# Three loads moved ahead of the entry barrier, and a 16 KB load cut into four

## The chip, the cores and the metric

The kernel runs on one core of a Trainium2 chip. The time is the device time of one execution in microseconds (us). "Span" is the time from the first to the last instruction in the profile; in the profiled runs it is 2.0 us (before) shorter than the device time. The engines are called PE (matmuls), DVE, ACT, POOL and SP; SP issues loads and stores, POOL issues the loads that cast fp32 to fp16. A load has "landed" when the last of its completions has come in. The granted clock is the share of its full clock that the record shows PE to have been allowed.

Almost all executions of this kernel agree within 1.5%. A few are some per cent longer (slow); they are used for nothing that concerns the time.

## The reference

Four batches of 12480 tokens of 128 numbers go through an attention block with 32 inducing points, then through a two-layer network with an exact GELU:

```
h   = softmax(scale * inducing @ x.T) @ x      # per batch: 32 x 128
y   = softmax(scale * x @ h.T) @ h             # per batch: 12480 x 128
out = gelu(y @ w_in) @ w_out                   # 49920 x 128, fp32
```

x is 25.6 MB and so is out, both fp32 in DRAM. The inducing points are 32 rows of 512 bytes, the weights 2 MB.

## The kernel before

What matters here is the start. POOL and SP issue the first loads; PE turns the inducing points (`indT`), runs eight warm-up matmuls ("fillers"), and then transposes the first tiles of x. Everything that PE does with x comes after the inducing points.

```python
blank = consts.tile([128, 512], FP16)
nc.vector.memset(blank, 0.0)

x_first = sb.tile([128, 32, 128], FP32, tag="o", bufs=OBUFS)
x_pair = x_tile(units[0][0])
src = units[0][0].rows_of(x_rows)
nc.sync.dma_start(out=x_first[:, :16, :], in_=src[:, :16, :])     # SP, 1 MB, no cast
nc.gpsimd.dma_start(out=x_pair[:, 16:, :], in_=src[:, 16:, :])    # POOL, casts, 512 KB written
a_load(units[0][2])                                               # POOL, casts, 1 MB written

identity = consts.tile([128, 128], FP32)
make_identity(nc, identity)                                       # on POOL
...
ind_s = consts.tile([M, C], FP32)
nc.sync.dma_start(out=ind_s, in_=inducing)                        # SP, 16 KB
indT_ps = ps.tile([C, M], FP32, tag="sc", bufs=3)
nc.tensor.transpose(indT_ps, ind_s, identity[:M, :M])
...
dim = ps.tile([128, 512], FP32, tag="sc", bufs=3)

def fill():
    nc.tensor.matmul(dim, blank[:, :128], blank, start=True, stop=True)
...
p_fill = None
for i in range(FILLERS):                                          # FILLERS = 8
    p_fill = plan.add((-1, 0), {"PE": 0.427}, lambda e: fill(), [p_fill])
```

Later loads of x are issued by POOL as buffers come free; stores of results are issued by SP.

The kernel's source does not show the entry barrier; the program built from it does. A barrier is a point that no engine passes before all of them have reached it. It is made of semaphores, counters that engines raise and wait for, and of drains: a drain is an instruction that is meant to hold its engine until earlier work is done. In front of all the code above stand, on each engine:

```
ACT, PE, DVE, SP:  Drain   (then: gather += 1)
                   EventSemaphore  wait release >= 1
POOL:              Memset x4       (small constants)
                   Drain
                   EventSemaphore  wait gather >= 4
                   EventSemaphore  release += 4
```

So POOL opens the barrier, and only after its own drain. (The profile shows the drains and these waits in this order on each engine.)

## Time and profile before

| | before |
|---|---|
| device time | 134.59 us (median; 134.44 to 135.2 in 5 runs) |
| span of the profiled run | 132.8 us |
| barrier open for the other engines | 0.7 us |
| PE has the inducing points | 6.43 us |
| first transposes of x | 10.03 us |
| last store issued | 122.6 us |

The profile's lines read: start in us, duration in us, engine, line of the kernel, operation, output<-input, count, and in brackets the idle time before and what ended it. `SPq` and `POOLq` are what the sequencer of that engine does. From the timeline of the kernel before, its first 12 us:

```profile
0.35 0.10 POOL L1130 MEMSET const-uint8-127<- 128x1 uint8 x1
0.75 1.28 ACT L355 ACT_TABLE_LOAD   x1 [0.75 <-PEq L1130]
0.75 0.38 SPq L285 DMA_DIRECT2D x_first<-in_x_dram  x1
1.19 0.42 SPq L295 DMA_DIRECT2D ind_s<-in_inducing_dram  x1
1.24 0.71 POOL L286 DMA_DIRECT2D xh<-in_x_dram  x1 [0.79 <-POOLq L1130]
1.95 0.53 POOL L277 DMA_DIRECT2D xh<-in_x_dram  x1
...
3.01 1.07 POOL L277 DMA_DIRECT2D xh<-in_x_dram  x2
...
6.43 0.28 PE L297 MATMUL indT_ps<-identity,ind_s 32*128 32x32 f32 x1 [6.43 <-DMA ind_s<-in_inducing_dram]
6.65 3.59 PE L349 MATMUL dim<-blank 128*128 128x512 f16 x8
...
10.03 2.07 PE L367 MATMUL tr<-identity_h,xh 128*128 128x128 f16 x32
```

The barrier opens at 0.7 us, SP issues x_first at once and the inducing points right behind it, and PE waits for those until 6.43 us. POOL's line for a load lasts 0.5 to 0.7 us, although the data comes many microseconds later. The Trainium skill ("Perfetto Trace Analysis", Per-engine timelines, DMA Instruction — SWDGE (GPSIMD)) says why: the profile ends such a line when the descriptors are written, not when the data has moved. This trace agrees: the first of POOL's loads, 0.71 us long from 1.24 us, landed at 8.58 us.

The table of stretches for the same kernel: the stretch in us and its length, then the busy time of PE, PE's weight loads, DVE, ACT and POOL (with counts), the granted clock, the DMA share (1 is all 16 DMA engines busy) and GB/s:

```profile
12.00:15.00 3.00, 1.34 (x28) 0.63 (x27) 1.67 (x4) 1.98 (x5) 0.53 (x1) 1.00 1.05 218
15.00:17.00 2.00, 2.00 (x46) 1.79 (x46) 1.25 (x2) 0.00 (x0) 0.00 (x0) 1.00 0.96 201
94.00:106.00 12.00, 10.19 (x142) 4.80 (x139) 10.92 (x32) 9.76 (x26) 7.63 (x8) 1.00 1.01 425
122.60:132.80 10.20, 0.00 (x0) 0.00 (x0) 0.24 (x2) 0.00 (x0) 0.00 (x0) 0.50 0.60 249
```

The DMA engines are never idle between 4 and 128 us. (218 GB/s of casting loads is the same work as 425 GB/s of stores: fp32 is read, half the bytes are written.) After the last store is issued, at 122.6 us, 10.2 us go by: the queue still holds the stores before it.

### The profile page before, as it was taken

How to read it: one execution, taken by the hardware profiler on the slowest of the kernel's cores; microseconds unless marked ns; L12 is line 12 of the kernel's file. 1: busy time of each engine (PE TensorE's matmuls, PEld its weight loads, DVE VectorE, ACT ScalarE, POOL GpSimd, SP SyncE). 2: the span in 40 equal slices, each digit the busy share in tenths (PEclk: the TensorE clock that was granted, in tenths of full speed). 3: DMA queues.
4: the chain of work that ended last, by engine and by line, in shares of the span. 5: the costliest groups of instructions: out<-in, count | busy, mean ns of one | idle time of the engine just before them, and what ended most of it. 6: DMA issues, size and time to landing. Idle time of an engine off the chain costs nothing. (4 is left out here: it accounts for less than half of the span.)

```text
span 132.8 us, 3490 instructions
## 1 busy us (share of the span) xinstructions
PE 97.3 (73%) x1365; PEld 56.6 (43%) x1365; DVE 93.4 (70%) x266; ACT 76.2 (57%) x173; POOL 65.3 (49%) x85
## 2 busy tenths in 40 slices
PE   0098678449999999999697979957988779295000
PEld 0036545349465556665363555624544424131000
DVE  1086557323699998999999489749989999998000
ACT  3004273316866879598878458967779759174000
POOL 6920131119344646894824409914167999556000
PEclk9999999965899999999999999999999999955555
DMA  4999999999999999999999999999999999999970
GB/s 123 302 223 215 217 200 220 212 220 210 220 205 220 215 200 313 333 398 367 299 318 348 266 227 324 321 412 425 430 423 426 415 437 413 411 434 425 421 300 15
DMA packets 5666, 40.17 MB, mean 303 GB/s; under 512 B 624, under 2 KB 1936, under 8 KB 2192
## 3 DMA queue, kind: packets, MB, share of 16 engines
q0 software_dynamic: 2848, 13.30, 49.5%
q1 hardware_dynamic: 2800, 26.63, 48.3%
q8 instruction: 11, 0.18, 0.5%
q14 instruction: 7, 0.06, 0.1%
HBM read 27.67 MB, written 25.56 MB: 401 GB/s over the span
## 5 line engine op out<-in xcount | busy, mean ns | idle before, releaser
L686 POOL TENSOR_TENSOR pair<-pair,rr 128x512 f32<-128x512 f32 x29 | 30.3, 1056 | 29.1 <-ACT pair L355 19.9
L670 PE MATMUL at<-q,e 128*128 128x512 f16 (+1 forms) x104 | 33.5, 389 | 7.2 <-DVE o L701 2.4
L367 PE MATMUL tr<-identity_h,xh 128*128 128x128 f16 x392 | 29.3, 227 | 2.3 <-DMA xh<-in_x_dram 2.1
L701 DVE TENSOR_TENSOR pair<-at,rr 128x512 f32<-128x512 f32 x41 | 26.8, 679 | 3.1 <-DMA out_dram<-pair 1.6
L367 PEld LDWEIGHTS <-xh 128*128 128x128 f16 x392 | 24.5, 102 | 7.6 <-issue 3.5
L355 ACT ACTIVATE xT<-tr 128x1024 f16<-128x1024 f16 (+1 forms) x17 | 16.7, 981 | 19.1 <-PE tr L367 19.1
L353 DVE COPY xT<-tr 128x1024 f16<-128x1024 f16 (+1 forms) x35 | 21.9, 644 | 7.0 <-PE tr L367 6.7
L355 ACT ACTIVATE pair<-at 128x512 f32<-128x512 f32 x29 | 17.2, 598 | 3.1 <-PE at L670 1.7
L628 ACT ACTIVATE e<-s 128x512 f16<-128x512 f32 (+1 forms) x28 | 15.2, 563 | 6.4 <-PE s L616 5.2
L277 POOL DMA_DIRECT2D xh<-in_x_dram x15 | 8.3, 556 | 21.5 <-DMA xh<-in_x_dram 14.3
L393 ACT ACTIVATE e<-s 128x512 f16<-128x512 f32 (+1 forms) x28 | 15.2, 543 | 5.4 <-PE s L381 5.0
L670 PEld LDWEIGHTS <-e 128*128 128x128 f16 (+1 forms) x104 | 8.9, 105 | 11.5 <-issue 8.5
L415 PE MATMUL hun<-xh,e1t 128*32 128x128 f16 x392 | 10.5, 222 | 3.2 <-DVE e1t L407 3.0
L562 POOL TENSOR_TENSOR pt<-pt 128x512 f32<-128x512 f32 (+4 forms) x20 | 12.0, 601 | 1.5
L407 DVE STREAM_TRANSPOSE e1t<-e 128x256 int32<-128x256 int32 (+1 forms) x28 | 11.0, 399 | 2.2 <-ACT e L393 2.2
L381 PE MATMUL s<-xT,indT 128*32 128x512 f16 (+1 forms) x108 | 10.5, 376 | 1.6 <-ACT xT L355 0.8
L415 PEld LDWEIGHTS <-e1t 128*32 128x32 f16 x392 | 6.3, 96 | 11.5 <-DVE e1t L407 9.0
L701 DVE TENSOR_TENSOR o<-at,rr 128x512 f32<-128x512 f32 (+1 forms) x19 | 10.2, 558 | 0.9 <-PE at L670 0.7
L686 POOL TENSOR_TENSOR o<-o,rr 128x512 f32<-128x512 f32 x8 | 8.2, 1044 | 4.0 <-ACT o L355 2.3
L616 PE MATMUL s<-xT,hT 128*32 128x512 f16 (+1 forms) x100 | 9.7, 391 | 0.1
L640 PEld LDWEIGHTS <-e 128*128 128x128 f16 (+1 forms) x104 | 5.6, 99 | 5.0 <-issue 1.3
L640 PE MATMUL r<-strand,e 128*128 128x4 f16 (+1 forms) x104 | 6.9, 168 | 0.2 <-ACT e L393 0.2
(72 smaller groups left out, 93.0 us busy)
## 6 DMA issues: line engine op xcount, KB each, us to landing
out_dram<-pair SPq DMA_DIRECT2D x9, 2048.0 KB, 15.0
xh<-in_x_dram POOLq DMA_DIRECT2D x11, 1024.0 KB, 28.0
out_dram<-o SPq DMA_DIRECT2D x6, 1024.0 KB, 7.5
x_first<-in_x_dram SPq DMA_DIRECT2D x1, 1024.0 KB, 5.4
xh<-in_x_dram POOLq DMA_DIRECT2D x1, 512.0 KB, 7.3
w_in_h<-in_moe_w_in_dram POOLq DMA_DIRECT2D x1, 512.0 KB, 17.5
w_out_h<-in_moe_w_out_dram POOLq DMA_DIRECT2D x1, 512.0 KB, 19.5
out_dram<-o SPq DMA_DIRECT2D x4, 96.0 KB, 12.4
```

Source lines behind the costliest of these rows:

```text
L353: nc.vector.tensor_copy(out=out, in_=in_)
L355: nc.scalar.activation(out=out, in_=in_, func=AF.Copy)
L367: nc.tensor.transpose(tr[:, c - c0, : u.p], xh[: u.p, c, :], identity_h[: u.p, : u.p])
L393: nc.scalar.activation(out=e1[: u.p, : u.nc // 2, :, :], in_=s1[: u.p, : u.nc, :].rearrange("r (a b) i -> r a i b", b=2), func=AF.Exp, sca ...
L407: nc.vector.transpose(out=pairs(e1t)[: u.p, :n], in_=pairs(e1)[: u.p, :n])
L415: nc.tensor.matmul(bt.hun[32 * j : 32 * j + 32, :], e1t[: u.p, c // 2, :, c % 2], xh[: u.p, c, :], start=u.idx == 0 and c < 4, stop=c + 4 ...
L562: nc.gpsimd.tensor_tensor(out=bt.pt[:, :, :, :half], in0=bt.pt[:, :, :, :half], in1=bt.pt[:, :, :, half : 2 * half], op=ALU.add,)
L628: nc.scalar.activation(out=e2[: u.rows, : u.cols], in_=s2[: u.rows, : u.cols], func=AF.Exp, scale=SCALE,)
L640: nc.tensor.matmul(r2[: u.p, ci, : u.nj], e2[: u.rows, ci * u.p : (ci + 1) * u.p], strand[: u.rows, : u.nj], start=True, stop=True,)
L670: nc.tensor.matmul(at[: u.p, : u.nj, :], e2[: u.rows, ci * u.p : (ci + 1) * u.p], bt.q[: u.rows, : u.nj, :], start=True, stop=True,)
L686: nc.gpsimd.tensor_tensor(out=part, in0=part, in1=rr2[: u.p, ci, : u.nj].unsqueeze(2).broadcast_to([u.p, u.nj, 128]), op=ALU.mult,)
L701: nc.vector.tensor_tensor(out=ov[: u.p, ci, :, :], in0=at[: u.p, : u.nj, :], in1=rr2[: u.p, ci, : u.nj].unsqueeze(2).broadcast_to([u.p, u. ...
```

## The change

The intent: the first three loads need nothing that the barrier protects, so let SP and POOL issue them before it, and have the DMA engines start earlier. The inducing points come in four transfers of 8 rows instead of one of 32.

```diff
     ind_s = consts.tile([M, C], FP32)
-    nc.sync.dma_start(out=ind_s, in_=inducing)
+    for m in range(0, M, M // 4):
+        nc.sync.dma_start(out=ind_s[m : m + M // 4], in_=inducing[m : m + M // 4])
@@ at the end of the kernel
+    nc.at_finalize(loads_ahead)
     return nc
+
+def loads_ahead(nc):
+    entry, body = nc.main_func.blocks[:2]
+    head, rest = list(entry.instructions), list(body.instructions)
+    for engine, n in ((mybir.EngineType.SP, 1), (mybir.EngineType.Pool, 2)):
+        moves = [i for i in rest if i.engine == engine][:n]
+        for i in moves:
+            assert isinstance(i, mybir.InstDMACopy)
+            rest.remove(i)
+        at = min(
+            k for k, i in enumerate(head)
+            if i.engine == engine
+            and isinstance(i, (mybir.InstDrain, mybir.InstMemset))
+        )
+        head[at:at] = moves
+    entry.instructions, body.instructions = head, rest
```

The moved loads land in front of the first drain or memset of their engine: on SP in front of its drain, on POOL in front of its four memsets, and so in front of its drain too.

More of the change, by code (lines that the diff above doesn't have):

```diff
@@ L977 @@
         general(tc, x, moe_w_in, moe_w_out, out, ind_s, identity)
+    nc.at_finalize(loads_ahead)
     return nc
+def loads_ahead(nc):
[7 more added lines that the diff above has]
+        at = min(
+            k
+            for k, i in enumerate(head)
+            if i.engine == engine
[3 more added lines that the diff above has]
+    entry.instructions, body.instructions = head, rest
 def general(tc, x, moe_w_in, moe_w_out, out, ind_s, identity):
```

## The prediction

> **What bounds the kernel now.** The DMA engines, end to end. The table of stretches shows a DMA share of 0.96 to 1.12 from 4 to 128 us; PE, DVE and ACT are busy 73%, 70% and 57% of the span (busy table). With casting loads counted at source size, the trace's DMA packets move 410 to 430 GB/s in every 2 us from 4 to 128 us, except 48 to 50 us (about 330). Outside it: the first packet starts at 1.76 us, 2 to 4 us run at about 285 GB/s, and one slow engine trails from 128 to 131 us. The chain of waits ends at 122.7 us; the span, 132.8 us, ends with the stores.
>
> Bytes issued less bytes moved leave at least 1.1 MB of stores queued whenever the next is issued after 94 us (2.5 us at 425 GB/s, an estimate). Moderate delays of the compute are absorbed; only the DMA engines' start counts.
>
> **What the change does, costed.**
> - SP: the 1 MB load of x_first starts at 0.75 us, after the barrier. Ahead of it, it can start when SP's register moves are done, at about 0.25 us. Its first packet came 1.0 us after issue, so I expect it at 1.25 us: gain 0.5 us.
> - POOL: its two load issues (0.71 and 0.53 us, timeline) now precede its memsets and drain. They start 0.6 us after POOL's barrier step now, so I expect them from 0.25 to 0.8 us, and the barrier released at 1.9 to 2.5 instead of 0.68 us. ACT's table load (1.28 us) and DVE's first memset slide into idle time: ACT first computes at 11.7 us, PE at 6.4 us.
> - Inducing points: one issue of 0.42 us at 1.19 us becomes four, from about 2.0-2.5 to 3.7-4.2 us. Now the rows sit behind x_first, ahead of POOL's loads, and PE gets them at 6.4 us. After the change POOL's loads are probably queued first. The Trainium skill ("DMA: Bandwidth & Descriptors", Queues, rings and completion order) says each engine takes turns between queues by packet; here the turns are long: the store issued at 45.6 us sent its first packet at 49.5 us. POOL's first load needs eight packets of 0.33 us per engine, 2.6 us. So I expect the inducing points at 6.5 to 8 us, not sooner, and the first transposes of x (10.0 us now, after 3.6 us of fillers) at 10 to 11.7 us.
>
> **On the critical path.** Only the 0.5 us of earlier DMA. The late inducing points are absorbed: PE waits for loads again at about 18.6 and at 29.0 us (1.4 us), and those come 0.5 us earlier.
>
> **Predicted time.** 134.59 - 0.5 = 134.1 us, range 133.4 to 135.0. Faster by over 2%: 0.02; within 2%: 0.94; slower by over 2%: 0.04.
>
> **What would show it right.** Timeline: x_first issued at about 0.25 us, barrier and ACT table load after 1.9 us. First packets near 1.25 us. Waits: PE's wait for the inducing points ends between 6.4 and 8 us. Stretches: DMA share about 1 from 4 us to the end; last store issued within 1 us of now; span 132.3 us.
>
> **What would make it wrong.** If the four small transfers wait two turns behind POOL's loads (the second has packets of 0.63 us, 5 us a turn), they land after 12 us, the compute falls 6 us behind, the store queue runs dry and the time rises by 2 to 3 us. If they land sooner than now, nothing more is gained. If SP's load can't start early, the gain is nil.

## More of the kernel before

The instructions of the entry barrier have one line number of their own. The view of that line (operation, count, then least, median and greatest duration in ns, first and last start in us) shows the drains:

```profile
L1130 ACTq DRAIN  x1: 8/8/8, 0.1 to 0.1; - x1
L1130 SPq DRAIN  x1: 7/7/7, 0.3 to 0.3; - x1
L1130 POOLq DRAIN  x1: 186/186/186, 0.3 to 0.3; - x1
```

They are short: POOL's took 186 ns, the others 7 to 10 ns.

## The result, and the profile after

| | before | after |
|---|---|---|
| device time, median of 5 runs | 134.59 us | 142.36 us (141.42 to 143.08) |
| span of the profiled run | 132.8 us | 139.8 us |
| barrier open for the other engines | 0.7 us | 13.3 us |
| PE has the inducing points | 6.43 us | 19.06 us |
| first transposes of x | 10.03 us | 22.66 us |
| last store issued | 122.6 us | 132.5 us |

The ratio is 1.0568 (95% interval 1.051 to 1.0626): slower by over 5%. Ratios here are the mean time of one kernel's fast runs over that of the other's fast runs of the same rounds, so not quite the ratio of the medians.

The timeline of the changed kernel, the lines that answer to those above:

```profile
0.26 0.39 SPq L285 DMA_DIRECT2D x_first<-in_x_dram  x1
0.75 0.72 POOL L286 DMA_DIRECT2D xh<-in_x_dram  x1 [0.75 <-issue]
1.46 0.54 POOL L277 DMA_DIRECT2D xh<-in_x_dram  x1
...
2.09 0.12 POOL L1154 MEMSET const-uint8-127<- 128x1 uint8 x1
13.33 0.20 POOL masks.py:197 MEMSET identity<- 128x128 f32 x1 [11.12 <-POOLq L1154]
13.34 1.36 SPq L298 DMA_DIRECT2D ind_s<-in_inducing_dram  x4
13.34 1.28 ACT L358 ACT_TABLE_LOAD   x1 [13.34 <-PEq L1154]
...
13.95 1.07 POOL L277 DMA_DIRECT2D xh<-in_x_dram  x2
...
19.06 0.28 PE L300 MATMUL indT_ps<-identity,ind_s 32*128 32x32 f32 x1 [19.06 <-DMA ind_s<-in_inducing_dram]
19.28 3.59 PE L352 MATMUL dim<-blank 128*128 128x512 f16 x8
22.66 2.41 PE L370 MATMUL tr<-identity_h,xh 128*128 128x128 f16 x32
```

The three loads do start early: x_first at 0.26 us instead of 0.75 us. Then no engine computes or issues anything between 2.2 and 13.3 us. The view of the barrier's line shows what held it:

```profile
L1154 ACTq DRAIN  x1: 8/8/8, 0.1 to 0.1; - x1
L1154 SPq DRAIN  x1: 123/123/123, 0.7 to 0.7; - x1
L1154 POOLq DRAIN  x1: 11832/11832/11832, 1.3 to 1.3; - x1
```

POOL's drain now lasts 11.83 us, from 1.26 to 13.09 us. POOL's second load, issued at 1.46 us, landed at 12.97 us. The view of DMA issues between 1.4 and 2.05 us (size, us from issue to landing) has it:

```profile
xh<-in_x_dram POOLq DMA_DIRECT2D x1, 1024.0 KB, 11.5
```

SP's drain stands behind SP's load in the same way and took 0.12 us, although that load landed only at 5.68 us.

The table of stretches of the changed kernel shows two holes in the DMA engines' work that were not there before:

```profile
12.00:15.00 3.00, 0.00 (x0) 0.00 (x0) 0.50 (x2) 1.28 (x1) 1.55 (x4) 1.00 0.02 4
15.00:17.00 2.00, 0.00 (x0) 0.00 (x0) 0.00 (x0) 0.00 (x0) 2.00 (x5) 1.00 0.93 103
100.00:112.00 12.00, 11.18 (x158) 5.66 (x157) 11.09 (x27) 9.65 (x28) 6.00 (x6) 1.00 0.62 255
132.50:139.80 7.30, 0.00 (x0) 0.00 (x0) 0.25 (x2) 0.00 (x0) 0.00 (x0) 0.50 0.69 274
```

The first hole is at 12 to 17 us: the two early loads are done, POOL issues its next one only at 13.95 us, and its first packets start at 15.21 us. The second is at 100 to 112 us: the compute, late since the start, has no result ready to store. To put numbers on it, I took the bytes of the DMA packets in a stretch (casting loads at source size), divided by 425 GB/s, and subtracted that from the length of the stretch. This is the DMA time lost:

| stretch | before, us lost | after, us lost |
|---|---|---|
| 0 to 6 us (start) | 2.63 | 2.23 |
| 6 to 20 us | 0.0 | 4.25 |
| 20 to 90 us | 0.76 | 0.22 |
| 90 us to the last store's issue | 0.0 | 5.34 |
| last store's issue to the end | 4.14 | 2.51 |
| sum | 7.50 | 14.55 |

The sums differ by 7.05 us and the spans by 7.06 us. They must, since both kernels move the same bytes; what the table tells is where the time went. The gain that was hoped for is in the first row: 0.4 us.

### The profile page after: what moved, and what is told of

The parts are those of the page before. It is cut to its first block, busy times and chain, and to the rows that moved or that the text cites. A ratio compares the mean times of both kernels' runs of the same rounds, so it can differ in the third digit from the quotient of the medians.

```text
span 139.8 us, 3494 instructions
## 1 busy us (share of the span) xinstructions
PE 96.9 (69%) x1365; PEld 56.7 (41%) x1365; DVE 93.5 (67%) x266; ACT 76.1 (54%) x173; POOL 65.8 (47%) x85
## 5 line engine op out<-in xcount | busy, mean ns | idle before, releaser
L673 PEld LDWEIGHTS <-e 128*128 128x128 f16 (+1 forms) x104 | 8.9, 105 | 11.7 <-issue 8.7
L384 PE MATMUL s<-xT,indT 128*32 128x512 f16 (+1 forms) x108 | 10.2, 366 | 1.7 <-ACT xT L358 0.8
L704 DVE TENSOR_TENSOR o<-at,rr 128x512 f32<-128x512 f32 (+1 forms) x19 | 10.2, 559 | 0.9 <-PE at L673 0.7
```

Source lines behind the costliest of these rows:

```text
L384: nc.tensor.matmul(s1[32 * j : 32 * j + 32, : u.nc, :], indT, xT[:, :, 32 * j : 32 * j + 32], start=True, stop=True,)
L673: nc.tensor.matmul(at[: u.p, : u.nj, :], e2[: u.rows, ci * u.p : (ci + 1) * u.p], bt.q[: u.rows, : u.nj, :], start=True, stop=True,)
L704: nc.vector.tensor_tensor(out=ov[: u.p, ci, :, :], in0=at[: u.p, : u.nj, :], in1=rr2[: u.p, ci, : u.nj].unsqueeze(2).broadcast_to([u.p, u. ...
```

## The experiments

Theory D: POOL's drain waits until the loads that POOL issued before it have landed; POOL opens the barrier, so the whole program starts some 12.6 us late. Rival S: the four small transfers cost the time. Rival B: any load in flight at the barrier holds it. All experiments gave correct results.

### e1: the three loads ahead, the inducing points in one transfer

```diff
-    for m in range(0, M, M // 4):
-        nc.sync.dma_start(out=ind_s[m : m + M // 4], in_=inducing[m : m + M // 4])
+    nc.sync.dma_start(out=ind_s, in_=inducing)
```

> The three loads ahead of the barrier, the inducing points in one transfer again. Theory D (POOL's drain in front of the barrier waits until its own two early loads have landed, and everything behind the barrier starts some 12.7 us late): the barrier is released at 13.3 us as in the change; the time stays at 138.5 to 142.5 us. Rival S (the four small transfers cost the time, because they take turns behind POOL's loads): the time falls to 134 to 135 us. A mix: if the split adds 3 us of the wait (PE waited to 19.06 us, though the points were issued from 13.3 us), PE's wait now ends at 15.5 to 16.5 us and the time is about 139 to 140 us.

Measured: 137.46 us (three fast runs, 137.24 to 137.56, one slow), ratio 1.022 (1.0143 to 1.0296). The barrier opens at 13.0 us, as in the change. The barrier's drain and the start of PE in the profile of e1:

```profile
L1153 POOLq DRAIN  x1: 11584/11584/11584, 1.3 to 1.3; - x1
```

```profile
14.83 0.28 PE L299 MATMUL indT_ps<-identity,ind_s 32*128 32x32 f32 x1 [14.83 <-DMA ind_s<-in_inducing_dram]
15.04 3.31 PE L351 MATMUL dim<-blank 128*128 128x512 f16 x8
18.19 1.95 PE L369 MATMUL tr<-identity_h,xh 128*128 128x128 f16 x32
```

The drain stays at 11.6 us without the split. One transfer that was issued at 13.09 us was with PE at 14.83 us; four, issued from 13.34 us, at 19.06 us. The time lies below everything that had been expected for theory D and for a mix (138.5 to 142.5 us): the barrier is as late as theory D says, but the split has a larger share than was allowed for. So the time of the change has two parts: about 3.2 us from the late barrier (137.46 against 134.27 us, the median of before in these rounds), and about 4.9 us (142.36 less 137.46 us, different rounds) that the split adds when the barrier is late. In the account of DMA time lost, e1 has 4.14 us between 6 and 20 us, like the change, but only 1.34 us from 90 us to the last store's issue (5.34 us in the change): what the split adds is the second hole.

### e2: only the split

```diff
 # the kernel before, with
+    for m in range(0, M, M // 4):
+        nc.sync.dma_start(out=ind_s[m : m + M // 4], in_=inducing[m : m + M // 4])
```

> Only the inducing points in four transfers, no load ahead. Theory D: 134.3 to 135.5 us, the barrier released at 0.7 us; PE's wait for the points may end later than the 6.4 us of before (up to 9 us), and the queue of stores absorbs that. Rival S: 138 us or more.

Measured: 134.86 us, ratio 1.0028 (0.9968 to 1.0089). PE had the points at 7.69 us instead of 6.43 us, and the time did not notice. Rival S falls as the root: the split alone costs nothing.

### e3: only SP's load ahead

```diff
-    for engine, n in ((mybir.EngineType.SP, 1), (mybir.EngineType.Pool, 2)):
+    for engine, n in ((mybir.EngineType.SP, 1),):
 # inducing points in one transfer
```

> Only the SP load of x_first ahead of the barrier, POOL's loads behind it, the inducing points in one transfer. Theory D: SP's drain does not wait for its load (it took 0.12 us in the change), so the barrier is released by 1.2 us, first data packet at about 1.25 us instead of 1.76 us, time 134.0 to 134.4 us. Rival (any load in flight holds the barrier): released at about 6 us, time 137 us or more.

Measured: 134.48 us, ratio 1.0004 (0.9954 to 1.0055). The barrier opened at 0.96 us with SP's load in flight, and SP's drain took 0.12 us again. Rival B falls: a load that SP issued does not hold the barrier. The first data packet came at 1.30 us, as expected, but the expected gain (0.2 to 0.6 us) did not show.

### e4: POOL's loads after its drain, still ahead of the barrier's semaphores

```diff
             if i.engine == engine
-            and isinstance(i, (mybir.InstDrain, mybir.InstMemset))
+            and isinstance(i, mybir.InstDrain)
         )
+        at += engine == mybir.EngineType.Pool
         head[at:at] = moves
 # inducing points in one transfer
```

> SP's load ahead as in the change, POOL's two loads placed after POOL's drain but before the two semaphore steps of the barrier; the inducing points in one transfer. Theory D: the drain finds nothing in flight and is short (about 0.2 us), the barrier is released between 0.7 and 2.5 us, time 133.8 to 134.6 us. Rival B (it is the barrier as such, or loads ahead of it, whatever the drain): released at 13 us, time 139 to 142 us.

Measured: 134.09 us (seven runs, 133.81 to 135.19), ratio 0.9967 (0.992 to 1.0014). From the view of the barrier's line in e4, and its timeline:

```profile
L1154 POOLq DRAIN  x1: 188/188/188, 0.3 to 0.3; - x1
```

```profile
7.40 0.28 PE L299 MATMUL indT_ps<-identity,ind_s 32*128 32x32 f32 x1 [7.40 <-DMA ind_s<-in_inducing_dram]
```

The same loads, behind POOL's memsets and drain instead of in front of them, and the drain is back to 188 ns; the barrier opens at 1.61 us and the whole loss is gone. This is the experiment that settles the root: it is the order of POOL's loads and POOL's drain, not the loads' being ahead of the barrier. (The loads also pass the four memsets, but in the change those had ended at 2.21 us, with 10.9 us of drain still to come.)

### e5: only the smaller of POOL's two loads ahead of the drain

```diff
-    for engine, n in ((mybir.EngineType.SP, 1), (mybir.EngineType.Pool, 2)):
+    for engine, n in ((mybir.EngineType.SP, 1), (mybir.EngineType.Pool, 1)):
 # inducing points in one transfer
```

> Only POOL's first load (half the size of the second) ahead of its drain, with SP's load; the inducing points in one transfer. Theory D: the drain ends when that load has landed, so the barrier is released at 8.0 to 8.6 us (in e1, with both loads, 13.1 us; the first alone had landed at 7.9 us there), time 135 to 137 us. Rival (the drain has a fixed long cost once any POOL load precedes it): 13 us again, 137.5 us.

Measured: 137.23 us, ratio 1.0209 (1.0151 to 1.0267). The barrier's line, and the issue of that load (size, us from issue to landing):

```profile
L1153 POOLq DRAIN  x1: 6935/6935/6935, 0.8 to 0.8; - x1
```

```profile
xh<-in_x_dram POOLq DMA_DIRECT2D x1, 512.0 KB, 6.9
```

The load was issued at 0.75 us and landed at 7.68 us; the drain ended at 7.76 us. In e1 the second load landed at 12.72 us and the drain ended at 12.84 us. The drain follows the landing of the last load in front of it by about 0.1 us, wherever that is, so the rival's fixed cost falls. The time lay just above what was expected: POOL's second load now goes out only behind the barrier, and the DMA engines are short of work from 7 to 11 us (3.6 us lost between 6 and 20 us).

### e6: a POOL drain behind the barrier, that only POOL feels

```diff
     make_identity(nc, identity)
+    nc.gpsimd.drain()
 # otherwise the kernel before
```

> The kernel before with one POOL drain put in its body, behind the barrier, after the first two loads and the making of the identity. Nothing ahead of the barrier. Theory D: the drain lasts from about 3 us until the second load has landed at about 13.3 us, POOL's later loads are issued only then, the DMA engines run dry between about 12.5 and 15 us and the time rises by 2.5 to 4 us to 137 to 138.5 us, although the first transposes of x stay at 10 us. Rival (only the late start of the compute costs time, the late loads nothing): 134 to 135 us.

Measured: 137.96 us, ratio 1.0241 (1.0178 to 1.0304). The drain in the view of its line, POOL's next load, and two stretches:

```profile
L291 POOLq DRAIN  x1: 10465/10465/10465, 2.7 to 2.7; - x1
```

```profile
13.71 1.07 POOL L277 DMA_DIRECT2D xh<-in_x_dram  x2 [10.63 <-issue]
```

```profile
12.00:15.00 3.00, 1.27 (x21) 0.58 (x22) 1.92 (x4) 2.29 (x5) 1.29 (x3) 1.00 0.16 25
...
94.00:106.00 12.00, 10.98 (x160) 5.76 (x160) 11.08 (x28) 9.79 (x27) 6.25 (x7) 1.00 1.02 430
```

The drain needs no barrier to do this: it lasted from 2.74 to 13.21 us, and the load in front of it landed at 13.09 us. The first transposes of x stayed at 9.8 us, so the compute was on time; only POOL's later loads were late. That alone cost 3.3 us of span, and the first hole accounts for it: 3.5 us lost between 6 and 20 us, none during the stores. The queue of loads was emptied, and what is not moved then has to be moved later.

### e7 and e8: only the compute late

```diff
+    extra = [1] * 12          # e8: [1] * 30
     def fill():
         nc.tensor.matmul(dim, blank[:, :128], blank, start=True, stop=True)
+        while extra:
+            extra.pop()
+            nc.tensor.matmul(dim, blank[:, :128], blank, start=True, stop=True)
```

> The kernel before with 12 more warm-up matmuls on PE, so that only the compute starts late, by 5.1 us (first transposes at 15.2 us), and the loads stay as they are. If the queue of stores absorbs it (about 4 to 5 us, read from the change against e1): 134.3 to 135.5 us. If the compute is the bound from the start: 139 us or more.

> The same with 30 more warm-up matmuls: the compute alone 12.8 us late (first transposes at 22.8 us, as in the change), the loads on time. If about 4.6 us are absorbed, 142 to 144 us with the store queue dry at about 100 to 106 us; if the DMA bytes alone bound the time, 134 to 136 us.

The doses were smaller than planned. I had reckoned 0.43 us for a warm-up matmul, but only the first nine came every 0.43 us; from 3.8 us after the first one on they came every 0.22 us. The Trainium skill ("TensorE: Matmul & The Clock Gate", Part 1: The HAM clock gate) says that PE runs at half clock until it has been busy for about 3.4 us, half a microsecond more or less. These traces agree roughly: 3.8 us after the first warm-up matmul in e7 and e8, 2.9 us in e1. So the transposes of x began at 12.63 us in e7 (2.6 us late) and at 16.52 us in e8 (6.5 us late).

Measured: e7 134.86 us (three fast runs, one slow), ratio 1.0063 (0.9979 to 1.0148), not to be told from before. e8 139.12 us, ratio 1.0354 (1.0285 to 1.0423). Two stretches of e8:

```profile
98.00:107.00 9.00, 8.44 (x129) 4.35 (x118) 8.21 (x20) 6.74 (x18) 3.76 (x5) 1.00 0.62 255
...
129.60:137.10 7.50, 0.00 (x0) 0.00 (x0) 0.19 (x2) 0.00 (x0) 0.00 (x0) 0.50 0.65 260
```

In e8 all loads were on time (no more DMA time lost before 20 us than before), yet the same second hole opened at 98 to 107 us. So the compute's late start alone is enough to open the second hole. The size shows in when the last store is issued and how long the program runs on from there:

| | transposes of x from | last store issued | from there to the end | span |
|---|---|---|---|---|
| before | 10.0 | 122.6 | 10.2 | 132.8 |
| e7 | 12.6 | 122.7 | 10.0 | 132.7 |
| e6 | 9.8 | 126.5 | 9.5 | 136.1 |
| e8 | 16.5 | 129.6 | 7.5 | 137.1 |
| e1 | 18.2 | 128.4 | 7.3 | 135.8 |
| after | 22.7 | 132.5 | 7.3 | 139.8 |

(All in us, from the profiled run of each.) Where the DMA queue is full, the last store has to queue and 10 us follow it. Where it has run dry, 7.3 to 7.5 us follow. So, where no DMA time was lost at the start, a last store that is up to about 2.8 us late costs nothing: in e2 it was issued at 124.7 us, 2.1 us late, and the span was 132.3 us. Where the queue has run dry, what goes beyond that counts in full: after, 9.92 us late less 2.86 us is the 7.06 us of the span; e8, 6.95 us late less 2.63 us, 4.3 us. In e6 the queue was full and the span longer all the same, because of the hole at the start.

How late the last store is does not follow from the start of the compute alone: e7 began 2.6 us late and issued its last store 0.1 us late; e1 began 1.7 us later than e8 and issued its last store 1.1 us earlier. What lies between was not tested, nor was the full delay of 12.6 us with the loads on time.

### e9: the change with POOL's loads after its drain, split included

```diff
 # the change, with e4's edit of the place; four transfers of 8 rows
```

> The change as it is, four transfers of the inducing points included, but POOL's two loads placed after its drain (as in e4). If the drain is the root and the split only costs what it does because the late barrier puts it against POOL's large packets: barrier released at about 1.6 us, PE gets the inducing points at 8 to 10 us, time 134.0 to 135.3 us. If the split has a cost of its own of 4 to 5 us (change against e1): 138 to 139 us.

Measured: 133.98 us (three fast runs, one slow), ratio 0.9984 (0.9942 to 1.0025). From its view of waits (who waited for what: us in total, times, longest us):

```profile
PE indT_ps L300 <- DMA ind_s<-in_inducing_dram: 9.6, 1, 9.6
```

The four transfers made PE wait to 9.65 us instead of the 7.40 us of e4, and that was absorbed. The split costs time only where the late barrier has used up the slack.

### e10: as e4, and the inducing points issued by ACT ahead of its drain

```diff
-    nc.sync.dma_start(out=ind_s, in_=inducing)
+    nc.scalar.dma_start(out=ind_s, in_=inducing)
-    ((mybir.EngineType.SP, 1), (mybir.EngineType.Pool, 2))
+    ((mybir.EngineType.SP, 1), (mybir.EngineType.Activation, 1), (mybir.EngineType.Pool, 2))
 # with e4's edit of the place
```

> As e4, and the inducing points (one transfer) issued by ACT ahead of its drain, so that they go beside x_first instead of behind it. PE should have them at 3 to 5 us, the first transposes of x at 8 to 9 us, set by PE's fillers and DVE's setup. If the DMA engines bound the time: 133.6 to 134.4 us, no more than 0.5 us gained. If an earlier compute is worth its microseconds: 132.5 us or less.

Measured: 133.88 us (six runs, 133.47 to 135.18), ratio 0.9954 (0.9922 to 0.9986). This is the only version whose interval lies below 1: it beats the kernel before by about 0.5%, and the change by 6% (median against median, different rounds). The start of PE in its profile:

```profile
2.98 0.29 PE L299 MATMUL indT_ps<-identity,ind_s 32*128 32x32 f32 x1 [2.98 <-POOL identity masks.py:199]
3.20 3.60 PE L351 MATMUL dim<-blank 128*128 128x512 f16 x8
8.30 3.43 PE L369 MATMUL tr<-identity_h,xh 128*128 128x128 f16 x32 [1.51 <-DMA xh<-in_x_dram]
```

PE now waits for the identity, not for the points, and later for x itself. Which of the two, the earlier DMA start or the earlier compute, gave the half per cent was not separated. Its profiled run was the slowest of the six (135.18 us), so its lines show the start, not the gain.

### e11: the change with two transfers of 16 rows

```diff
-    for m in range(0, M, M // 4):
-        nc.sync.dma_start(out=ind_s[m : m + M // 4], in_=inducing[m : m + M // 4])
+    for m in range(0, M, M // 2):
+        nc.sync.dma_start(out=ind_s[m : m + M // 2], in_=inducing[m : m + M // 2])
```

> The change with two transfers of 16 rows instead of four of 8. Theory T (the rows that reach the engines after POOL's third load, whose first packets started at 15.2 us in the change, take turns with its packets of 8 KB; those before it do not): the second transfer is issued at about 13.7 us, its rows go at about 14.7 us, before POOL's packets; PE has the points by 15.0 to 15.6 us, time 137 to 138.3 us, as e1. Rival F (each further small transfer costs a fixed time, 4.2 us for three): about 16.3 us and 139 us.

Measured: 137.91 us (three fast runs, 137.27 to 137.92; two slow), ratio 1.0255 (1.0216 to 1.0295), as e1. PE had the points at 15.13 us (the profiled run fell in the slow state; only this early time is used from it). Theory T predicted 15.0 to 15.6 us, rival F 16.3 us.

The packets of the change's trace fit theory T. The four transfers were issued at 13.34, 13.74, 14.07 and 14.40 us. Of the 32 rows, 22 had gone when POOL's first 8 KB packet started at 15.21 us, two went at 16 us, and the last eight only at 17.27 to 17.93 us, with their completions at 17.93 to 18.6 us. A completion there came about 0.65 us after its row, and most POOL packets there took 0.62 to 0.68 us (the first ones up to 1.88 us). The Trainium skill ("DMA: Bandwidth & Descriptors", Queues, rings and completion order) says that each DMA engine takes turns between queues, packet by packet; that agrees with these intervals. The trace does not say which engine moved which packet, so the turns themselves are inferred.

### e12: as e4, with the inducing points ahead on SP

```diff
-    ((mybir.EngineType.SP, 1), (mybir.EngineType.Pool, 2))
+    ((mybir.EngineType.SP, 2), (mybir.EngineType.Pool, 2))
 # with e4's edit of the place; one transfer
```

> As e4, with SP's one transfer of the inducing points also ahead of SP's drain: issued at about 0.6 us, behind x_first and ahead of POOL's loads. PE has them at 5.7 to 6.3 us instead of 7.4 us in e4; time 133.7 to 134.5 us, not to be told from e4 if the DMA engines bound it.

Measured: 134.37 us, ratio 0.9994 (0.9957 to 1.0031). PE had the points at 5.88 us, as expected, and the time is that of before.

## Why the prediction was wrong

1. **The step that failed** is "the barrier released at 1.9 to 2.5 instead of 0.68 us". I had seen that POOL's loads would stand in front of its drain, and I costed them with the length of their lines in the timeline, 0.71 and 0.53 us. The drain does not wait for those lines to end but for the data to land. It took 11.83 us; the barrier opened at 13.3 us. e5, e6, e1 and the change show drains that end about 0.1 us after the last landing, at 7.76, 13.21, 12.84 and 13.09 us; e4 shows 188 ns with the order reversed.
2. **x_first at 0.25 us, first packet at 1.25 us**: right (0.26 and 1.27 us). SP's drain did not mind SP's load.
3. **"The inducing points at 6.5 to 8 us"** assumed the barrier of point 1. e9 has that barrier (1.61 us) and the four transfers, and PE got them at 9.65 us; e4, with one transfer, at 7.40 us. The direction was right and the size too small for four. With the real barrier it was 19.06 us.
4. **"Moderate delays of the compute are absorbed", 2.5 us of queue**: right in size. About 2.8 us of late last store were free (e8, e1, after); e7's 2.6 us at the start cost nothing that could be measured. But 12.6 us is not moderate. The passage on what would make the prediction wrong foresaw the mechanism (compute 6 us behind, store queue dry, 2 to 3 us); the measured price of 6.5 us was 4.3 us of span (e8).
5. **"Only the DMA engines' start counts"** was incomplete. The queue of loads has to stay filled as well: POOL's later loads, 10 us late, cost 3.3 us by themselves (e6). The prediction had no term for it, because it let POOL go on at 2.5 us.
6. **A gain of 0.5 us** from the earlier start: the DMA time lost in the first 6 us fell by 0.4 us (2.63 to 2.23), but as device time it was not resolved in e3, e4 and e12 (ratios 1.0004, 0.9967 and 0.9994, all intervals across 1). Only e10 gained clearly, 0.5%.

The profiled runs of e3, e4, e10 and e12 issued their last store 2.8 to 3.7 us later than before, although their transposes of x began within 1 us of before or earlier. Their traces show where they lost it. The sixth store, issued at 74.6 us before, went out 0.4 to 1.2 us earlier in these four, and the seventh (83.5 us before) 4.0 to 5.0 us later. In between, the record of the granted clock has PE at half its clock: from 72.9 to 86.5 us in e3, e4 and e10 and from 73.7 to 83.9 us in e12, where before has the full clock. The same stretch, before and in e4:

```profile
73.00:87.00 14.00, 12.77 (x181) 8.04 (x181) 10.38 (x33) 9.78 (x20) 8.55 (x11) 1.00 1.02 286
73.00:87.00 14.00, 12.08 (x114) 7.64 (x114) 6.58 (x14) 5.69 (x12) 3.98 (x5) 0.52 1.03 290
```

PE is busy almost as long and gets 114 matmuls done instead of 181. So the early start was kept for 70 us and then hidden by the clock, in runs that were among the slowest of their versions (135.41, 135.19 and 135.18 us for e3, e4 and e10). That is read from four traces; no run set the clock, and why it was halved there stays open. It is also open why the store issued at 45.6 us in the kernel before sent its first packet only at 49.5 us.

## What to carry to other kernels

An instruction that moves work ahead of a barrier has to be placed with the barrier's own drain in view: a drain on POOL behind POOL-issued loads waits for their data, so put such loads after the drain. (All of POOL's loads here cast; a plain one was not tried.) Do not take the length of a POOL load's line for its duration; look at when it lands. In a kernel that keeps the DMA queue full, a delay is free only as far as the queue reaches (here a last store that is about 2.8 us late), and both queues count, the loads' at the start and the stores' at the end.

## What the Trainium skill lacked or had wrong

- No page says whether a drain waits for loads still in flight (the nearest words, in "PSUM — Partial Sum Buffer", have it wait until its engine is idle). On POOL it waits for the loads that POOL issued before it. Measured: 11.83, 11.58, 10.47 and 6.94 us, each ending about 0.1 us after the last landing; 188 ns where the loads follow the drain. It would belong to "DMA: Bandwidth & Descriptors" or "GPSIMD Engine Reference".
- Nor does a page say that the drains of SP and ACT differ: SP's took 0.12 us directly behind a 1 MB load that landed at 5.68 us, ACT's 0.145 us behind the inducing points that landed at 2.84 us (e10).
- "VectorE: DVE Perf Modes" (The DRAIN you can't avoid) tells of two kinds: the flush after a DVE operation, and the runtime's own drains at a kernel's start and end, about 12 ns and constant on all five engines. It lacks a third, the drains of the program's own entry barrier, which look alike and are not constant: ACT, DVE and PE took 8 to 10 ns, SP 7 ns, but SP 123 ns and ACT 145 ns behind a load, and POOL 186 ns behind four memsets and up to 11.83 us behind loads.
- "Perfetto Trace Analysis" (Per-engine timelines, Sequencer-only Instruction) draws a drain with the sequencer and semaphores as its only actors. For POOL a third counts, the loads in flight: see the first point.
